# A convolution-and-MLP kernel: the blocked transform becomes a two-stage transform with partition shuffles, the gate becomes one plus a scaled convolution, and the first row passes its norm by itself

## Chip, cores, metric

One core of a Trainium2 chip. Times are microseconds (us) of device time of that core. The experiments ran on two chips: taps_kept, both_half, tail_split and dum_halves on one, the others on another, each beside the kernel before. Words used below: an eviction copies a result of TensorE from PSUM, its output memory, to SBUF, the main memory on the chip; a shuffle is a DMA that moves data between SBUF partitions; a dummy is a matmul whose result nobody reads; TensorE is cold while it runs at half its clock; a row is one of 16 groups of 128 positions. A run is called fast or slow: slow is over 1.5% above the fastest run of the same kernel. A ratio below is the mean time of one kernel's fast runs over the mean of the other's fast runs of the same rounds, so it is not quite the ratio of the medians quoted beside it.

## The reference, cut to what matters

```python
def reference(A_q, A_k, A_v, A_shift_k, A_ssm_k, A_ssm_D, B_x, B_w1, B_b1, B_w2, B_b2):
    # S = 2048, D = 448, F = 1792, bfloat16
    x = A_q
    q = layernorm(x)                                   # over D
    k_shift = sum over 4 taps of shifted k * shift_k   # per channel
    kv = k_shift * v
    y = irfft(rfft(kv, 2S) * rfft(ssm_k, 2S))[:S] + kv * ssm_D   # causal convolution along S
    h = x + q * y
    u = gelu(einsum("bsd,sf->bdf", layernorm(h), w1) + b1)
    return h + transpose(einsum("bdf,fs->bds", u, w2) + b2)
```

The kernel computes the convolution with matmuls against tables of sines, the MLP (which mixes along S) with two chains of 224 matmuls.

## The kernel before

The sequence is cut in 16 tiles of 128 positions and four blocks of 512. Each block is transformed to 512 frequencies, the products for each pair of blocks are summed on TensorE with identity matrices, and each output tile is transformed back, from one block's products or two.

```python
def emit_forward(...):                        # L834: 2 tables x 4 x 4 matmuls per block and signal
    for tab, ... in ((NC_t, ...), (NSf_t, ...)):
        for phi in range(NPHI):
            for tp in range(TPB):
                ... e.matmul(bank(bk), tab[:, tp, 128*phi:128*phi+128], sig[:, tile, :], ...)
            ... e.copy / e.activation(out=dst_ap, in_=bank(bk))     # ScalarE, 448 columns each

def emit_products_b(b):                       # for every block pair c + j = b
    for hf in range(2):
        for c in range(b + 1):
            # four VectorE products, then eight identity matmuls (L908 to L917)
            ... e.matmul(bank(bre), ident,  mset[:, 0, q, :], ...)
            ... e.matmul(bank(bre), nident, mset[:, 1, q, :], ...)
            # [cut]

def emit_inverse_T(T):                        # L945: 8 or 16 matmuls per output tile
    # [cut]

def emit_combine_T(T):
    ... t1s = kv - bank(bk)                   # VectorE, from PSUM (L962)
    ... t2s = t1s * qs2                       # qs2: normalised x, read back from HBM (L964)
    ... hs  = t2s + xs2                       # L966
    # hs goes out to HBM and comes back for the last addition
    # row sums and squares on ScalarE, scale on ScalarE (L970 to L987)
    # [cut]

def emit_gelu(q, fc):                         # two ScalarE passes, three VectorE passes, a sigmoid
    # [cut]
```

## Time and profile before

| | before |
|---|---|
| time, median of 3 runs | 296.19 us (295.44 to 296.56) |
| profiled span | 295.9 us |
| TensorE, VectorE, ScalarE, GpSimd busy | 78%, 60%, 54%, 11% |
| front and convolution, up to the first MLP stretch | 0 to 158 us |
| rest of the inverse, rows, first MLP product, GELU | 158 to 246.5 us |
| second MLP product, store | 246.5 to 295.9 us |

The prediction shows the stretches before 158 us and after 246.5 us. The one between, in the same columns (start:end, length, busy us with instruction counts of TensorE, its weight loads, VectorE, ScalarE and GpSimd, then granted clock, DMA share, GB/s), of the kernel before:

```profile
158.00:246.50 88.50, 73.93 (x344) 34.40 (x345) 38.46 (x111) 46.47 (x100) 10.52 (x26) 0.90 0.55 182
```

The clock of 0.90 and the 14.6 us in which TensorE is idle say that this stretch waits. The chain of waits (start, us, what) says for what, a row that is read back from HBM and weights:

```profile
172.24 9.92 DMA qs<-out_dram
...
215.29 6.37 DMA XB<-in_B_w_dram
...
233.83 4.52 DMA XB<-in_B_w_dram
```

### The profile page before, as it was taken

Reading aid. Unit: us, or ns where it says so; the run is one execution under the profiler, and the core shown is the slowest. Engines: PE = TensorE matmul, PEld = TensorE weight load, DVE = VectorE, ACT = ScalarE, POOL = GpSimd, SP = SyncE. Lnnn points to the kernel's source line nnn. Section 1 sums busy time; section 2 is a strip of 40 time slices with the busy share of each in tenths; the row PEclk is TensorE's granted clock in tenths of the full one; section 3 lists DMA queues with packets and bytes.
Section 4 is the critical chain, followed back from the end, with each engine's and each line's share of the span. In section 5 each row is a group of like instructions: output and inputs, shape, how many; then the busy total and the mean of one; then the engine's idle time right before and its main releaser. Section 6 shows DMA issues by size and latency. Waiting matters only on the chain.

```text
span 295.9 us, 3832 instructions
## 1 busy us (share of the span) xinstructions
PE 229.9 (78%) x1154; PEld 112.8 (38%) x1154; DVE 178.4 (60%) x426; ACT 159.4 (54%) x335; POOL 33.1 (11%) x81
## 2 busy tenths in 40 slices
PE   0024169999779999899928969759929999799995
PEld 0023124455325555445503425325514444345552
DVE  8959986685998974987187772442244124454131
ACT  2389266998753585867682683854656135610000
POOL 6001120000000032221223031321100000000000
PEclk9999999999979999999975989979987999999999
DMA  6721776658043333221220199436984420025322
GB/s 183 193 74 71 224 232 190 199 173 265 7 149 94 111 113 91 78 78 32 65 62 1 47 320 363 113 109 194 328 329 127 141 107 2 0 62 147 105 62 78
DMA packets 28552, 39.36 MB, mean 133 GB/s; under 512 B 3060, under 2 KB 23670, under 8 KB 28532
## 3 DMA queue, kind: packets, MB, share of 16 engines
q1 hardware_dynamic: 22100, 24.44, 27.5%
q10 hardware_dynamic: 6432, 14.68, 14.7%
q8 instruction: 9, 0.15, 0.2%
q14 instruction: 11, 0.09, 0.1%
HBM read 33.61 MB, written 5.51 MB: 132 GB/s over the span
## 4 chain that ended last, share of the span: by engine, by line
PE 44%; DVE 10%; DMA 8%; ACT 5%; issue 2%; POOL 1%; DVEq 1%; SPq 0%; ACTq 0%
PE ps_all L1046 13%; PE ps_all L1063 12%; PE ps_all L945 8%; PE ps_all L834 4%; DMA XB<-in_B_w_dram 4%; DMA qs<-out_dram 3%; PE ps_all L908 2%; PE ps_all L914 2%; PE ps_all L917 2%; PE ps_all L911 2%; DVE XB L888 1%; DVE XB L890 1%; DMA xs<-in_A_q_dram 1%; DVE XB L886 1%; DVE t1s L962 1%
## 5 line engine op out<-in xcount | busy, mean ns | idle before, releaser
L1046 PE MATMUL ps_all<-hn,XB 128*128 128x448 bf16 x224 | 50.3, 379 | 14.1 <-DMA XB<-in_B_w_dram 6.3
L1063 PE MATMUL ps_all<-XB,YB 128*128 128x448 bf16 x224 | 43.6, 353 | 2.5 <-DVE XB L1036 2.5
L1046 PEld LDWEIGHTS ps_all<-hn,XB 128*128 128x128 bf16 x224 | 22.5, 104 | 40.7 <-issue 13.9
L945 PE MATMUL ps_all<-XB,NC_t 128*128 128x448 bf16 x112 | 32.1, 364 | 1.8 <-ACT XB L924 1.1
L945 PE MATMUL ps_all<-XB,NSi_t 128*128 128x448 bf16 x112 | 32.3, 363 | 0.0
L752 PE MATMUL ps_all<-ident,XB 128*128 128x128 bf16 (+1 forms) x64 | 7.0, 293 | 31.7 <-DMA XB<-in_A_ssm_k_dram 17.3
L1063 PEld LDWEIGHTS ps_all<-XB,YB 128*128 128x128 bf16 x224 | 21.4, 98 | 24.3 <-DVE XB L1036 4.6
L834 PE MATMUL ps_all<-kv,NC_t 128*128 128x448 bf16 x64 | 19.9, 366 | 6.9 <-DVE t1s L962 6.9
L1066 DVE SCALAR_TENSOR_TENSOR osb<-ps_all,b2col,hs 128x448 bf16<-128x448 f32 x16 | 10.5, 681 | 21.6 <-PE ps_all L1063 21.6
L924 ACT CAST XB<-ps_all 128x448 bf16<-128x448 f32 x32 | 16.9, 530 | 10.8 <-PE ps_all L911 8.0
L834 PE MATMUL ps_all<-XB,NC_t 128*128 128x448 bf16 x64 | 21.3, 398 | 0.7 <-ACT XB L761 0.7
L840 ACT ACTIVATE YB<-ps_all,sc 128x448 bf16<-128x448 f32 x32 | 18.7, 632 | 4.8 <-PE ps_all L834 4.7
L844 ACT CAST YB<-ps_all 128x448 bf16<-128x448 f32 x32 | 16.6, 534 | 8.4 <-PE ps_all L834 8.3
L834 PE MATMUL ps_all<-kv,NSf_t 128*128 128x448 bf16 x64 | 19.9, 366 | 0.7 <-ACT YB L844 0.7
L790 DVE TENSOR_TENSOR XB<-XB,Wt 128x1792 bf16<-128x1792 bf16 x16 | 17.1, 1079 | 4.9 <-DMA XB<-in_A_k_dram 4.8
L834 PE MATMUL ps_all<-XB,NSf_t 128*128 128x448 bf16 x64 | 19.9, 352 | 0.0
L1029 DVE SCALAR_TENSOR_TENSOR XB<-XB 128x448 bf16<-128x448 bf16 x14 | 8.8, 625 | 15.9 <-ACT XB L1023 8.4
L752 PEld LDWEIGHTS ps_all<-ident,XB 128*128 128x128 bf16 (+1 forms) x64 | 5.7, 139 | 32.8 <-DMA XB<-in_A_ssm_k_dram 18.4
L821 ACT ACTIVATE qs<-xs,nm_x,rs_x 128x448 bf16<-128x448 bf16 x16 | 12.1, 760 | 9.3 <-DVE nm_x L818 9.0
L908 PE MATMUL ps_all<-XB,ident 128*128 128x448 bf16 x40 | 14.5, 364 | 3.1 <-DVE XB L896 2.8
L945 PEld LDWEIGHTS ps_all<-XB,NC_t 128*128 128x128 bf16 x112 | 11.2, 100 | 13.9 <-ACT XB L924 1.5
L970 ACT ACTIVATE junk<-hs 128x448 bf16<-128x448 bf16 x16 | 9.2, 575 | 12.5 <-DVE hs L966 5.6
(103 smaller groups left out, 386.3 us busy)
## 6 DMA issues: line engine op xcount, KB each, us to landing
XB<-in_B_w_dram ACTq DMA_DIRECT2D x32, 224.0 KB, 2.9
YB<-in_B_w_dram ACTq DMA_DIRECT2D x2, 3584.0 KB, 13.6
XB<-in_A_k_dram SPq DMA_DIRECT2D x15, 448.0 KB, 4.0
xs<-in_A_q_dram SPq DMA_DIRECT2D x32, 112.0 KB, 2.2
XB<-in_A_v_dram SPq DMA_DIRECT2D x16, 112.0 KB, 3.2
out_dram<-qs SPq DMA_DIRECT2D x16, 112.0 KB, 1.7
qs<-out_dram SPq DMA_DIRECT2D x16, 112.0 KB, 2.4
out_dram<-hs SPq DMA_DIRECT2D x16, 112.0 KB, 1.9
```

Of the source, the lines that this page charges most:

```text
L752: op("pe", lambda e, dst=dst, slot=slot, tt=tt, w=w: e.transpose(out=dst, in_=knat[0:w, slot, 128 * tt: 128 * tt + 128], identity=ident[0: ...
L790: op(E, lambda e: e.tensor_tensor(out=prod, in0=ktap[:, slot, :, :], in1=Wt, op=ALU.mult), reads=[r_ktap[slot], r_Wt], writes=[r_prod[ei]] ...
L821: op("act", lambda e: e.activation(out=qs[:, slot, :], in_=xs[:, slot, :], func=ACT.Identity, bias=nm_x[:, t:t + 1], scale=rs_x[:, t:t + 1 ...
L834: op("pe", lambda e, bk=bk, lhsT=lhsT, tile=tile, tp=tp: e.matmul(bank(bk), lhsT, sig[:, tile, :], start=(tp == 0), stop=(tp == TPB - 1)), ...
L840: op("act", lambda e, bk=bk, dst_ap=dst_ap, scl=scl: e.activation(out=dst_ap, in_=bank(bk), func=ACT.Copy, scale=scl), reads=[Rbank[bk], r ...
L844: op("act", lambda e, bk=bk, dst_ap=dst_ap: e.copy(out=dst_ap, in_=bank(bk)), reads=[Rbank[bk]], writes=[r_d], n=D)
L908: op("pe", lambda e, bre=bre, mset=mset, q=q, first=first: e.matmul(bank(bre), ident, mset[:, 0, q, :], start=first, stop=False), reads=[r ...
L924: op("act", lambda e, bk=bk, dst=dst: e.copy(out=dst, in_=bank(bk)), reads=[Rbank[bk]], writes=[r_Pst[pslot]], n=D)
L945: op("pe", lambda e, lhsT=lhsT, rhs=rhs, ti=ti: e.matmul(bank(bk), lhsT, rhs, start=(ti == 0), stop=(ti == n - 1)), reads=[r_l, r_r], writ ...
L1046: op("pe", lambda e, q=q, slot=slot, t=t: e.matmul(bank(q), w1s[:, slot, 128 * q: 128 * q + 128], hn[:, t, :], start=(t == 0), stop=(t == ...
L1063: op("pe", lambda e, fc=fc: e.matmul(bank(bk), w2sb[:, fc, 128 * T: 128 * T + 128], gT[:, fc, :], start=(fc == 0), stop=(fc == NFC - 1)), ...
L1066: op("dve", lambda e: e.scalar_tensor_tensor(out=osb[:, ob, :], in0=bank(bk), scalar=b2col[:, T:T + 1], in1=hs2[:, fs, :], op0=ALU.add, op ...
```

## The change

The intent is to take work from TensorE and the round trips from the rows.

- **Transform.** The positions are cut as s = 16 q + r. A first stage multiplies, for each residue r, 128 positions with a sine table (two matmuls, which make 896 columns in PSUM). Shuffle DMAs move the results between partitions inside SBUF, so that the residues lie on the partition axis; a second stage of half-size matmuls (64 stationary columns) finishes the transform. It is taken at odd half frequencies, so that one set of products, one per frequency, serves the causal convolution of the whole sequence, where ten block pairs were needed. The inverse mirrors this: half-size matmuls (64 rows), shuffles, a full-size last stage.
- **Gate.** h - mean = (x - m)(1 + r y) up to a constant of the row, which the following norm removes. So the last stage's PSUM goes through one pass, 1 + scale times convolution, and one combine.
- **First row at once.** Rows 0 and 1 each take a norm of their own, so that row 0 waits for no other; rows 2 to 15 go in pairs.
- Also: GELU is one ScalarE function; a planner chooses the order of instructions and which engine evicts; TensorE runs dummy matmuls in waits.

The diff rewrites nearly the whole file (some 2,000 lines); its core:

```diff
-    for t in range(NT): ... emit_forward / emit_products_b / emit_inverse_T
+def emit_stage1(src, o_src, T, o_T, tag):
+    for r in range(R):
+        for h in range(2):
+            op("pe", ... e.matmul(Pb(b, h), E[:, 2*r + h, :], src[:, r, :], ...))          # L933
+        op("act", ... copy of both banks, 896 columns)                                     # L943
+        for q_, a, b_, j0 in (("pool", 0, 112, 0), ("sp", 112, 128, 14)):
+            op(q_, ... e.dma_start(T[p0:p0 + 29:4, j0:...], WR[a:b_]))                     # L947, shuffle
+def emit_stage2(T, o_T, scale):
+    for jj ...: for h ...:
+        for c in range(2):
+            for par in range(2):
+                op("pe", ... e.matmul(PS[64*par:64*par+64, slot(c), 0:D],
+                                      FW[:, 64*c:64*c+64], T[:, j, h, :], ...))            # L964
+        evac(...)                                    # ScalarE or VectorE, L652 to L656
+def emit_products_i1():
+    op("dve", ... all four products of 448 columns in one tensor_tensor)                   # L1015
+    for t ...: for par in range(2):
+        op("pe", ... e.matmul(Pb(b, par), tab[P, :], M[P, xy, :], ...))   # P: 64 rows, L1027
+    evac(...); shuffle                                                                     # L1037
+def emit_i2():
+    op("pe", ... two matmuls per row)                                                      # L1104
+    op(FX, ... activation(out=A, in_=Pb(b), bias=1.0, scale=r))                            # L1111, gate
+    op("dve", ... A = (X - mean) * A)                                                      # L1118
+    # rows in groups GR = ((0, 1), (1, 1)) + pairs: a group of one takes bn_stats on VectorE,
+    # a group of two row sums with the combine, squares on ScalarE, arithmetic on GpSimd
-    dma(out2d <- hs); ... dma(hs2 <- out2d)
-    # six passes for GELU
+    op("act", ... activation(func=Gelu_apprx_tanh))                                        # L1193
```

## The prediction

> **What bounds the kernel now.** I read the head of the page first, then the stretches view, the groups, and last the chain of waits, where TensorE runs without a stop.
>
> ```profile
> span 295.9 us, 3832 instructions
> PE 229.9 (78%) x1154; PEld 112.8 (38%) x1154; DVE 178.4 (60%) x426; ACT 159.4 (54%) x335; POOL 33.1 (11%) x81
> ```
>
> TensorE is the busiest engine by 50 us, and idle for 66 us. The stretches view (start:end, length, busy us of PE, PEld, DVE, ACT and POOL, then clock, DMA share and GB/s) shows where, cut at the first and last transform and MLP matmuls:
>
> ```profile
> 0.00:40.50 40.50, 7.18 (x66) 5.82 (x66) 34.72 (x69) 21.56 (x39) 6.98 (x20) 1.00 0.54 160
> 40.50:158.00 117.50, 105.33 (x520) 51.20 (x520) 87.27 (x216) 83.06 (x183) 15.56 (x36) 0.96 0.38 114
> ...
> 246.50:292.50 46.00, 43.50 (x226) 21.33 (x223) 16.70 (x31) 8.28 (x15) 0.00 (x0) 1.00 0.23 68
> 292.50:295.90 3.40, 0.00 (x0) 0.00 (x0) 1.22 (x2) 0.00 (x0) 0.00 (x0) 0.81 0.21 68
> ```
>
> VectorE sets the first 40 us (tables, then taps), TensorE most of the convolution and the second MLP product; the last 3.4 us are eviction and store. The time per matmul is not its duration, as matmuls overlap; it comes from the chain:
>
> ```profile
> 261.67 30.83 PE ps_all L1063 x162
> ```
>
> 30.83/162 = 0.190 us. There are 256 forward, 160 identity-sum, 224 inverse and 448 MLP matmuls, 1,088 in all: 207 of the 230 busy us. The groups give the costs that I carry over (count, busy us, mean ns of one):
>
> ```profile
> L790 DVE TENSOR_TENSOR XB<-XB,Wt 128x1792 bf16<-128x1792 bf16 x16 | 17.1, 1079 | 4.9 <-DMA XB<-in_A_k_dram 4.8
> ...
> L924 ACT CAST XB<-ps_all 128x448 bf16<-128x448 f32 x32 | 16.9, 530 | 10.8 <-PE ps_all L911 8.0
> ...
> L962 DVE TENSOR_TENSOR t1s<-kv,ps_all 128x448 bf16<-128x448 bf16 x16 | 9.8, 616 | 2.3 <-PE ps_all L945 2.3
> ...
> L720 ACT ACTIVATE NSi_t<-XB,negpi 128x1024 bf16<-128x1024 f32 x4 | 4.5, 1137 | 2.7 <-DVE XB L719 2.7
> L725 DVE SCALAR_TENSOR_TENSOR XB<-XB 128x1024 f32<-128x1024 f32 x4 | 4.9, 1220 | 0.0
> ```
>
> The reader is to see a large SBUF product, a PSUM eviction on each engine, a table row and [...]VectorE work.
>
> **What the Trainium skill says.** "VectorE: DVE Perf Modes", The perf-mode tier table: a bf16 tensor_tensor in SBUF runs at twice the base rate, fp32 PSUM operands at the base rate. The trace agrees: 390 ns (L966) against 616 ns (L962) for 448 columns. "TensorE: Matmul & The Clock Gate", Part 3: matmuls on different row or column groups of the array run together. Nothing in this trace shows it; the new half-size matmuls rest on it. "DMA: Bandwidth & Descriptors", Why a DMA increments its semaphore by 16 and not by 1: a DMA uses the largest number of engines up to 16 that divides both outer sizes. The shuffles have outer sizes 112 and 8 (16 and 8 for the rest), so 8 engines each; no trace yet. "SBUF — State Buffer", A bandwidth-pool intuition that's wrong: a GpSimd DMA can starve while VectorE runs a two-port copy; the shuffles use that path, but beside them VectorE mostly multiplies or reads PSUM. Not shown here either.
>
> **The change, part by part.** It is nearly a rewrite. The blocked convolution (four blocks, products for every block pair) becomes one transform in two stages of 16 rows, a DMA shuffle between stages, and one product per frequency.
>
> TensorE: the 640 convolution matmuls become 66 first-stage, 68 tap-sum and weight-row, and 32 last-stage ones of full size, plus 128 half-column and 128 half-row ones, which I count in pairs as 128. That is 294 slots or 56 us in place of 122; 97 transposes and 66 clock-keeping dummies fill idle time. The MLP stays at 448. TensorE no longer sets the front; evictions do.
>
> Front, until the last stage can start (my sums):
> - VectorE only: table index work 6.5 (per half one 1,024-column row of 1.22 and about 2 us of faster integer rows); tap products 16 x 1.08 = 17.3; times v from PSUM, 896 columns, [...]1.08, x8 = 8.7; spectrum products 16 x 1.08 = 17.3; row statistics 16 x about 0.77 = 12.3 (estimate from 448 columns at base rate plus a short row); small 2. Sum 64.
> - ScalarE only: sines and table loads 7.7; first-stage evictions of 896 columns, [...]0.90, x32 = 28.9. Sum 37.[...]
> - Either: 48 evictions of 896 columns at a mean near 0.95 (ScalarE 0.90, VectorE 1.08) = 45.6; transposed kernel 6, weight rows 2, inverse tables 3.4. Sum 57.
> Total 158, so 79 us on each engine if both are always busy. I add 3 before either has real work, 3 for the last shuffle, which is a barrier, and 1 net for poor packing less the statistics that can follow later: **86 us**.
>
> In order: first stage of k from about 11 to 27 us, kv done near 41, first stage of u near 43, its shuffle near 46, then 39 us of second stages, products and inverse evictions.
>
> After that TensorE is the bound again: 32 + 448 = 480 matmuls x 0.190 = 91.2. The first normalised row takes a chain of some 4.5 us (0.4 matmuls, 0.7 gate, 0.7 combine, 0.8 statistics, 0.6 power as in L982's 601 ns, 0.5 scale, hops), of which 2 us is other last-stage work: 2.5 lost. Row loop stalls 1. Tail 3.4, as before. Sum **98 us**.
>
> The gate: (x-m)(1 + r y) differs from x + (x-m) r y by a row constant that the norm removes, so two VectorE rows and all q and h round trips through HBM go; per row two PSUM-to-output passes on VectorE (about 1.2 us) and a gate plus square with accumulator read on ScalarE (0.72 + 0.57 + 0.19 = 1.48) remain, under TensorE's 9 x 0.190 = 1.71. Passing the first row through at once brings the first MLP matmul forward by perhaps 1 to 2 us; it is in the 4.5. GELU drops from six passes to one (0.63) and is hidden.
>
> Bytes: the shuffles move 3 x 16 x 128 x 1,792 B = 11 MB in SBUF; HBM traffic falls from 39 to about 24 MB.
>
> 86 + 98 = **184 us**, 0.62 of before.
>
> **Rivals.**
> (a) Shuffles set the front. If 3.67 MB per shuffle went at 100 GB/s, the 37 us would outlast the 15 us of evictions that feed it, three times over: +25 to +60, 210 to 240 us. For: 1,792 B pieces, eight engines, descriptors written by GpSimd. Against: the page's GB/s row reaches 363, so half the engines should still pass 150, and consecutive shuffles can alternate halves.
> (b) Static order and semaphores leave VectorE and ScalarE 85% busy in place of 97%. The old kernel has VectorE at 34.7 of its first 40.5 us. That makes the front 93 to 95 and the time 192.
> (c) Weights come late. Half of w1 and all of w2, 11 MB, may only load after the last shuffle. At 304 GB/s (old trace, 169 to 186 us) they take 36 us and are hidden, as the second product starts some 52 us later; at 192 GB/s (204 to 246 us) 57 us, +5: 189.
> (d) The row loop goes at the pace of evictions, as seven of eight banks hold MLP sums and one is left: 2.2 us a row in place of 1.71 gives +8: 192.
> (e) VectorE rows that need nothing of each other overlap (two of L790 in 2.09, not 2.16) and the row statistics slide behind the last stage: front 80, time 177.
>
> **Range and chances.** (b), (c) and (d) each add 5 to 9 and may come together; (e) takes 7. I give 174 to 198 for 8 in 10. Even (a) stays far below 296, so faster is nearly certain: 0.98 faster, 0.01 same, 0.01 slower.
>
> **What would show it.** Right: last-stage matmuls start at 80 to 94 us; VectorE and ScalarE both over 85% busy from 10 us to there; from then to the end about 98 us with TensorE over 90%; 0.19 us a matmul in the MLP; half-size matmuls at about 0.1 us each. Wrong: VectorE waiting on a DMA for over 8 us in the second stages (a); TensorE waiting for w1 or w2 (c); row period over 2 us (d); half-size matmuls at 0.19, which would cost TensorE 24 us in the front, though under the evictions.

## The result

| | before | after |
|---|---|---|
| time, median of 4 runs each, same rounds | 296.38 us (295.44 to 297.94) | 189.75 us (188.61 to 191.89) |
| ratio of fast runs | | 0.638, 95% interval 0.634 to 0.642 |
| profiled span | 295.9 us | 187.1 us |
| convolution, up to where rows and MLP begin | 158.0 us | 87.7 us |
| rows, first MLP product | 88.5 us | 53.8 us |
| second MLP product and end | 49.4 us | 45.6 us |

The last three rows add up to the spans: of the 108.8 us gained, 70.3 come from the convolution, 34.7 from the rows and the first product, 3.8 from the end. The second stretch is not the same work in both: before, it also held 120 matmuls of the convolution (344 less the MLP's 224), some 23 us at 0.190; after, 32 of them, 6 us. So about half of the 34.7 is the transform's too (an estimate). The rest is near the 20.8 us of DMA waits shown above for the kernel before, which the changed kernel's chain does not have; only the gate's share was tested. One of the four runs of the changed kernel was slow (191.89 us). The result is correct.

The head of the page of the changed kernel:

```profile
span 187.1 us, 2824 instructions
PE 173.9 (93%) x1033; PEld 91.8 (49%) x1033; DVE 110.0 (59%) x181; ACT 97.2 (52%) x141; POOL 72.3 (39%) x176
```

TensorE's 93% is not what it seems. Matmuls overlap, their ends are modelled, and dummies count. The stretches say more (the same columns as before):

```profile
0.00:15.50 15.50, 14.12 (x99) 7.78 (x100) 12.72 (x22) 8.71 (x10) 10.76 (x50) 1.00 0.87 340
15.50:32.80 17.30, 14.15 (x69) 5.79 (x68) 15.43 (x19) 16.15 (x21) 13.85 (x25) 1.00 0.78 222
32.80:50.00 17.20, 16.20 (x93) 6.67 (x95) 14.52 (x15) 14.90 (x18) 13.73 (x24) 1.00 0.74 214
50.00:62.80 12.80, 11.24 (x96) 3.92 (x97) 11.01 (x12) 11.99 (x15) 2.27 (x9) 1.00 0.75 262
62.80:81.10 18.30, 16.69 (x154) 6.59 (x152) 17.62 (x20) 17.01 (x20) 7.82 (x14) 1.00 0.86 280
81.10:87.70 6.60, 6.57 (x34) 3.24 (x34) 6.28 (x21) 0.91 (x1) 6.11 (x13) 1.00 0.61 185
87.70:120.30 32.60, 31.36 (x160) 14.69 (x160) 21.47 (x62) 20.38 (x47) 17.74 (x44) 1.00 0.86 340
120.30:141.50 21.20, 21.20 (x114) 11.05 (x112) 0.00 (x0) 6.50 (x12) 0.00 (x0) 1.00 0.00 0
141.50:183.90 42.40, 42.37 (x224) 32.05 (x222) 10.25 (x15) 0.64 (x1) 0.00 (x0) 1.00 0.11 41
```

Two things are to be seen. From 15.5 to 81.1 us VectorE and ScalarE are both busy nearly all the time, yet so is TensorE: three engines at 82 to 96% in each stretch, and the view does not say which of them holds the others. From 81.1 to 87.7 us ScalarE stands still: it is the last shuffle, and all 34 TensorE instructions in that stretch are dummies. The chain of waits (start, us, what) shows the path from there on:

```profile
62.81 2.50 PE ps L1027 x24
...
81.13 6.61 PE ps L1047 x34
...
87.74 1.70 PE ps L1104 x8
...
120.31 21.19 PE ps L1213 x112
141.49 42.39 PE ps L1223 x224
```

The first line gives 2.50/24 = 0.104 us for a half-size matmul, the last two (21.19 + 42.39)/336 = 0.189 us for a full one. L1047 is the dummies. The groups that took the place of those shown before:

```profile
L943 ACT CAST arena<-ps 128x896 bf16<-128x896 f32 x32 | 26.6, 935 | 3.8 <-PE ps L933 1.9
...
L964 PE MATMUL ps<-arena 128*64 128x448 bf16 x128 | 16.4, 361 | 1.8 <-ACT arena L652 1.0
...
L1015 DVE TENSOR_TENSOR arena<-arena 128x1792 bf16<-128x1792 bf16 x16 | 16.4, 1082 | 0.0
...
L1027 PE MATMUL ps<-arena 64*128 64x448 bf16 x128 | 14.1, 351 | 1.3 <-DVE arena L1015 0.6
```

The mean of 351 ns for a half-size matmul is a duration with a modelled end, not a cost; the spacing of 0.104 us in the chain is the cost. And the shuffles, from the issues part of the page (count, KB each, median us from issue to landing):

```profile
arena<-arena POOLq DMA_DIRECT2D x48, 196.0 KB, 4.9
```

### The profile page after: what moved, and what is told of

The parts are those of the page before. It is cut to its first block, busy times and chain, and to the rows that moved or that the text cites. A ratio compares the mean times of both kernels' runs of the same rounds, so it can differ in the third digit from the quotient of the medians.

```text
span 187.1 us, 2824 instructions
## 1 busy us (share of the span) xinstructions
PE 173.9 (93%) x1033; PEld 91.8 (49%) x1033; DVE 110.0 (59%) x181; ACT 97.2 (52%) x141; POOL 72.3 (39%) x176
## 4 chain that ended last, share of the span: by engine, by line
PE 76%; ACT 8%; DVE 7%; DMA 3%; POOL 3%; issue 2%; ACTq 0%
PE ps L1223 23%; PE ps L1213 11%; PE ps L1203 10%; PE ps L1047 5%; PE ps L1027 5%; ACT arena L652 4%; PE ps L964 4%; DMA arena<-arena 3%; PE ps L1104 3%; PE ps L885 3%; PE ps L914 3%; PE ps L904 3%; POOL arena L947 3%; PE ps L933 3%; DVE arena L1015 2%
## 5 line engine op out<-in xcount | busy, mean ns | idle before, releaser
L1227 DVE SCALAR_TENSOR_TENSOR arena<-ps,arena 128x448 bf16<-128x448 f32 x16 | 10.9, 683 | 56.9 <-PE ps L1223 56.9
L1223 PE MATMUL ps<-arena 128*128 128x448 bf16 x224 | 42.5, 352 | 0.0
L1223 PEld LDWEIGHTS ps<-arena 128*128 128x128 bf16 x224 | 32.3, 144 | 10.1
L943 ACT CAST arena<-ps 128x896 bf16<-128x896 f32 x32 | 26.6, 935 | 3.8 <-PE ps L933 1.9
L652 ACT CAST arena<-ps 128x896 bf16<-128x896 f32 (+1 forms) x26 | 22.0, 908 | 2.6 <-PE ps L868 1.6
L1203 PE MATMUL ps<-arena 128*128 128x448 bf16 x112 | 23.0, 353 | 0.3 <-DVE arena L1159 0.2
L947 POOL DMA_DIRECT2D arena<-arena x32 | 19.2, 603 | 7.1 <-ACT arena L943 4.3
L1213 PE MATMUL ps<-arena 128*128 128x448 bf16 x112 | 21.4, 352 | 0.0
L1193 ACT ACTIVATE arena<-ps,arena 128x448 bf16<-128x448 f32 x14 | 8.2, 641 | 20.1 <-PE ps L1213 14.7
L879 DVE TENSOR_TENSOR arena<-arena 128x1792 bf16<-128x1792 bf16 x16 | 18.3, 1178 | 0.0
L964 PE MATMUL ps<-arena 128*64 128x448 bf16 x128 | 16.4, 361 | 1.8 <-ACT arena L652 1.0
L1111 ACT ACTIVATE arena<-ps,arena 128x448 f32<-128x448 f32 x16 | 11.2, 723 | 12.2 <-PE ps L1104 9.1
L1037 POOL DMA_DIRECT2D arena<-arena x16 | 9.5, 595 | 20.8 <-PE ps L964 15.6
L933 PE MATMUL ps<-arena 128*128 128x448 bf16 x64 | 16.0, 355 | 1.3 <-ACT arena L943 1.3
L885 PE MATMUL ps<-arena 128*128 128x448 bf16 x64 | 14.5, 354 | 2.5 <-ACT arena L943 1.9
L1015 DVE TENSOR_TENSOR arena<-arena 128x1792 bf16<-128x1792 bf16 x16 | 16.4, 1082 | 0.0
L1203 PEld LDWEIGHTS ps<-arena 128*128 128x128 bf16 x112 | 10.9, 98 | 11.1 <-DVE arena L1159 1.3
L1213 PEld LDWEIGHTS ps<-arena 128*128 128x128 bf16 x112 | 11.0, 98 | 10.2
L1027 PE MATMUL ps<-arena 64*128 64x448 bf16 x128 | 14.1, 351 | 1.3 <-DVE arena L1015 0.6
## 6 DMA issues: line engine op xcount, KB each, us to landing
arena<-in_B_w_dram SPq DMA_DIRECT2D x2, 1536.0 KB, 17.2
```

Source lines behind the costliest of these rows:

```text
L652: return e.copy(out=dst(), in_=src())
L879: op("dve", lambda e, W, T=T, i=i, r=r: e.tensor_tensor(out=T[:, i], in0=KH[:, r:r + 4, :], in1=WT, op=ALU.mult), r=[(o_KH + r * DB, 4 * D ...
L885: op("pe", lambda e, W, b=b, T=T, i=i, j=j: e.matmul(Pb(b, i), ID, T[:, i, j, :], start=(j == 0), stop=(j == 3)), r=[(o_ID, 256), (o + (i ...
L933: op("pe", lambda e, W, b=b, r=r, h=h, dl=dl: e.matmul(Pb(b, h), E[:, 2 * r + h, :], src[:, r, :], start=True, stop=not dl), r=[r_E(r), (o ...
L943: return e.copy(out=dst, in_=Ppair(b)) if W == "act" else e.tensor_copy(out=dst, in_=Ppair(b))
L947: shuf[tag + q_ + str(r)] = shuf[tag + q_] = op(q_, lambda e, W, w=w, p0=p0, a=a, b_=b_, j0=j0: e.dma_start(T[p0:p0 + 29:4, j0:j0 + (b_ - ...
```

## The experiments

The changed kernel ran again beside no_wk, no_pairing and gate_undone: 189.67 us median, ratio to before 0.6365 (0.6324 to 0.6406), two of six runs slow. All twelve kernels ran beside the kernel before. The column "against after" is (ratio - 0.6365) x 297.4 us. The intervals of the ratios are 0.003 to 0.008 wide to each side, and both ratios of a difference have one, so differences under 1.4 to 2.7 us, by run, are not told apart from zero: of the table, no_wk, no_pairing, taps_half and tail_split differ. A second caution: the planner chooses the order anew for each kernel. By the traces, VectorE and ScalarE keep their order in taps_kept, both_half, hw_last2 and no_late_dummies, and nearly in no_pairing; in no_wk, gate_undone, norm_pairs, tail_split and taps_half they do not, so what these show is the edit with its new order.

| run | ratio to before | against after |
|---|---|---|
| after_again | 0.6365 | |
| no_wk | 0.6456 | +2.7 us |
| no_pairing | 0.6441 | +2.3 us |
| gate_undone | none (two fast runs only) | about +6 us, by spans |
| norm_pairs | 0.6372 | +0.2 us |
| no_late_dummies | 0.6412 | +1.4 us |
| taps_half | 0.6561 | +5.8 us |
| hw_last2 | 0.6400 | +1.0 us |
| taps_kept | 0.6348 | -0.5 us |
| both_half | 0.6339 | -0.8 us |
| tail_split | 0.6465 | +3.0 us |
| dum_halves | one look | |

> The changed kernel unaltered, beside the variants of this call, so that effects of 1 to 3 us can be read on one chip. Every theory: 188 to 192 us, ratio to before 0.634 to 0.642; last stage starts at 87 to 89 us of the span.

The repeat gave spans from 186.1 to 190.1 us for one and the same kernel. Keep this spread in mind; its likely source appears under no_late_dummies and hw_last2.

### Are VectorE and ScalarE the bound of the front? taps_half, taps_kept, both_half

The main theory, the prediction's: the front is as long as the work of VectorE and ScalarE together. The test halves the tap products.

```diff
-  tensor_tensor(out=T[:, i],      in0=KH[:, r:r+4, :], in1=WT)          # four taps
+  tensor_tensor(out=T[:, i, 0:2], in0=KH[:, r:r+2, :], in1=WT[:, 0:2])  # two taps, wrong on purpose
-  matmul(..., ID, T[:, i, j, :])
+  matmul(..., ID, T[:, i, j % 2, :])
```

> Wrong result on purpose: each tap product of VectorE multiplies two of the four taps (half the elements, TensorE still sums four), which takes some 16 x 0.6 = 9.6 us out of VectorE before 47 us, and nothing else; the order of work is planned anew with the smaller cost. Theory A (the front is bounded by the sum of VectorE and ScalarE, which share the evictions): half of 9.6, so the last stage starts 3.5 to 5 us earlier and the whole is that much shorter. Theory B (latencies and the order of arrival set the front, VectorE's work is beside them): under 1.5 us. Theory C (VectorE alone is the bound): 7 to 9.6 us.

It was 5.8 us slower, which no theory had. The planner had been told the smaller cost and had made another order; the last stage started at 92.7 us, and VectorE was busy for only 4.6 of the 15.1 us from 31.9 to 47. The run says nothing on the bound, and something on how much the order weighs. So the planner's estimate was left as it was, which keeps the order:

> The halved tap products again (wrong result on purpose; 0.617 instead of 1.178 us each in the last run, so 16 x 0.56 = 9 us less of VectorE before 47 us), but with the order of all instructions kept exactly as in the changed kernel, since the run that planned anew came out 6 us longer. Theory A (VectorE and ScalarE together bound the front; with a fixed split ScalarE can't take any of the room that VectorE gets): the last stage starts 1 to 4 us earlier, whole -1 to -4 us. Theory B (neither is the bound; latencies are): within 0.8 us. Theory C (VectorE alone): -7 to -9 us. In all three the 6 us were the new order's; if this run is also longer, they belong to the products themselves.

Result: -0.5 us, and the last stage started at 87.70 us instead of 87.74. VectorE's busy time before 62.8 us fell from 53.7 to 46.2 us, so 7.5 us of work went and nearly nothing came of it. Then ScalarE's evictions of the input's first stage were halved as well:

```diff
   # in the first-stage eviction, on top of the tap products
+  if tag == "u":
+      return e.copy(out=dst[:, 0], in_=Pb(b, 0))     # one bank of two, wrong on purpose
```

> As the run before, and ScalarE's evictions of the first stage of the input copy only one of their two banks (wrong result on purpose, order kept): some 16 x 0.4 = 6.4 us less of ScalarE between 30 and 50 us on top of VectorE's 9. Theory A (the two together bound the front): the last stage starts 5 to 8 us earlier than in the changed kernel, clearly more than with the tap products alone. Theory B (latencies and shuffles bound it): within 1.5 us. Theory C (VectorE alone): no more than the tap products alone gave.

Result: -0.8 us. The evictions fell from 924 to 532 ns (medians). By the busy time of the whole run, 7.8 us were gone from VectorE and 5.2 from ScalarE, some 13 us from the two "binding" engines. Theory A expected the last stage 5 to 8 us earlier; it came 0.3 us earlier, at 87.45 us. (The first stage of both runs happened to start 0.3 to 0.4 us late, too little to matter.) The chain of waits and the stretches of this run:

```profile
8.00 13.09 DMA arena<-in_A_k_dram
...
61.88 1.17 PE ps L1029 x10
...
87.45 1.70 PE ps L1106 x8
```

```profile
32.80:50.00 17.20, 16.63 (x103) 7.35 (x103) 11.89 (x17) 11.35 (x21) 13.24 (x26) 1.00 0.81 225
```

L1029 and L1106 are the inverse product and the last stage, L1027 and L1104 of the changed kernel: the first starts 0.93 us earlier, the second 0.29. In the 17.2 us stretch VectorE and ScalarE are now busy for 11.9 and 11.4 us, a third idle, and TensorE does only slightly more. **Theory A falls for the part of the front up to 50 us**, with this order and this split of the evictions; theory B has the size right. (A plan that makes use of the freed time was not found: taps_half planned anew and was slower.) What holds instead can be read in the changed kernel's chain of waits for that time; no edit tested it:

```profile
23.35 6.47 DMA arena<-arena
...
32.82 0.93 PE ps L885 x4
33.75 1.05 PE ps L933 x5
34.80 0.76 PE ps L885 x4
```

Until 32.8 us it goes through GpSimd's issues of shuffles and the landing of one (6.47 us), which frees a buffer that the next first-stage eviction needs. From 32.8 us TensorE runs tap sums (L885) and first stages (L933) with no gap until 42.3, at 0.19 us each; all TensorE pieces of the chain between 32.8 and 50 add up to some 13 of 17 us. In the run with both halved, the chain before that is the landing of k from HBM at 21.1 us and of one more shuffle at 32.8 us. So the front up to 50 us is held by loads, shuffles and TensorE in turn, with VectorE and ScalarE busy beside them.

From 50 to 81.1 us the chain passes through seven evictions of ScalarE in a row (5.78 us) and VectorE's products, and from 62.8 on VectorE has no more than 0.7 us of room. That the two are the bound there is read, not tested, and TensorE is not out of the path: no_pairing, below, makes only its half-size matmuls dearer, and its last stage starts 1.3 us later.

### Dummies: no_wk and no_late_dummies

The front begins with dummies among the transposes of the convolution kernel. Nine of them are taken away:

```diff
-  N_WZ, N_WI, N_W0, N_WK, N_WJ = 34, 6, 9, 3, 8
+  N_WZ, N_WI, N_W0, N_WK, N_WJ = 34, 6, 9, 0, 8
```

> The nine dummy matmuls placed between the transposes of the kernel sequence are left out (the first nine at the start stay). In the profile the first stage of the sequence only starts at 14.3 us, where I had 11, and the last sixteen transposes wait until 12.4 us for the PSUM bank that the dummies hold. Theory A (the dummies hold a bank back and so delay the start, and the front is a queue of VectorE and ScalarE work that begins with the start): first stage 1.5 to 2.5 us earlier, total 1 to 2.5 us shorter, 187 to 189. Rival B (the dummies keep the TensorE clock up, so without them the early matmuls run slower): granted clock under 0.98 or matmuls over 0.2 us before 30 us, total the same or up to 2 us longer. Rival C (the transposes wait for their loads): no change.

The first stage did start earlier, at 13.5 instead of 14.3 us. But the stretches of this run show the clock:

```profile
0.00:15.50 15.50, 13.05 (x82) 6.93 (x83) 13.08 (x23) 8.02 (x9) 10.78 (x50) 0.94 0.86 344
15.50:31.90 16.40, 15.95 (x74) 6.64 (x75) 13.19 (x16) 15.55 (x19) 13.14 (x23) 0.85 0.70 200
```

0.94 and 0.85, against 1.00 in the changed kernel; matmuls around 14 us took 0.55 us instead of 0.35. The trace's clock records put the half clock at 13.5 to 20.4 us. The first stage gained 0.8 us, and the whole lost 2.7; all six runs were at a mean clock of 0.98 to 0.99. The dummies pay, though the new order may have a part in the 2.7.

A clock that halves is what the Trainium skill describes in "TensorE: Matmul & The Clock Gate", Part 1: The HAM clock gate: the array's clock is halved after an idle window of about 3.4 us, and the window runs freely, so the same kernel may be cold for a while in one run and not in the next. The traces agree with the halving (0.37 instead of 0.19 us a matmul, see hw_last2), with the idle window in no_late_dummies below (half clock 4.2 us after TensorE's last matmul), and with the difference from run to run. TensorE was not idle in no_wk, though: before 13.5 us its timeline shows it waiting for 0.6 us at most. What ran from 4.9 us on were transposes and matmuls of one row; how far these count as work for the clock, no run tests.

The late dummies (34 during the last shuffle, 14 among the first rows) were the other test:

```diff
-  N_WZ, N_WI, N_W0, N_WK, N_WJ = 34, 6, 9, 3, 8
+  N_WZ, N_WI, N_W0, N_WK, N_WJ = 0, 0, 9, 3, 0
```

> Takes away the 48 dummy multiplications behind the inverse products (34 in the 6.6 us in which the last shuffles land, 14 among the first rows); the early ones stay. Theory A (they keep the clock up, as the early ones turned out to do): the granted clock falls under 0.95 somewhere after 81 us and the first last-stage and MLP matmuls run at more than their 0.19 us for a few us: +1.5 to +4 us in all. Theory B (they only fill a wait): no change of the clock after 81 us, the last stage's start stays at 87.7 us (within 0.5), and the whole within 0.7 us of the changed kernel.

```profile
81.10:87.70 6.60, 2.21 (x20) 0.62 (x16) 6.60 (x19) 3.10 (x4) 5.58 (x12) 0.85 0.71 211
87.70:94.50 6.80, 3.83 (x11) 1.60 (x12) 4.05 (x10) 2.79 (x4) 2.10 (x5) 0.50 0.56 166
```

By the clock records the half clock lasts from 85.7 us, 4.2 us after the last inverse product ended (81.5), to 95.9; the last stage of this run starts within it, at 90.67 us, and its longest matmul takes 582 instead of 363 ns. From the start of the last stage to the end it took 100.2 us (99.4 in the changed kernel). Theory A is right in mechanism: the clock falls. Its cost is not told apart from zero: +1.4 us by the ratio, whose interval is 2.4 us to each side; the trace shows 0.8 in the tail. (The profiled run is a slow one, 192.75 us; but the fast runs too list mean clocks of 0.955 and 0.973, where the changed kernel's list 0.98 to 1.00.) The profiled run was longer by 3.8 us mainly for another reason: its first stage started at 16.3 us, 2 us late, in a part of the order that the edit does not touch.

### The last shuffle: hw_last2 and tail_split

The barrier from 81.1 to 87.7 us looked like the easiest gain. First the route: the last four groups' shuffles from SyncE, the small pieces of the last two from ScalarE.

```diff
-  op(q_, lambda ...: e.dma_start(TZ[...], TU[...]))                       # q_: GpSimd, SyncE for the small piece
+  op(("act" if j >= 14 and q_ == "sp" else "sp") if j >= 12 else q_, lambda ...: e.dma_start(TZ[...], TU[...]))
```

> The shuffles of the last four of 16 groups go out from SyncE and (the small pieces of the last two) ScalarE instead of GpSimd; bytes, sources and targets are the same. In the changed kernel the last ones are issued at 82.6 and 83.2 us and land at about 87.3, and nothing but dummies runs on TensorE from 81.1 to 87.7. Theory A (the 4.7 us from issue to landing belong to GpSimd's route): the last stage starts 1 to 2.5 us earlier, whole -1 to -2.5 us. Theory B (the bytes over eight DMA engines take that long by any route): within 0.5 us. Theory C (SyncE's own issues, 0.67 us each, stand in a line): 0.5 to 2 us longer.

The changed kernel's last issues and this run's, each from its timeline (start, us, engine, line):

```profile
82.55 1.27 POOL L1037 DMA_DIRECT2D arena<-arena  x2
```

```profile
79.76 6.88 SPq L1037 DMA_DIRECT2D arena<-arena  x8
...
90.38 1.69 PE L1104 MATMUL ps<-arena 128*128 128x448 bf16 x8 [0.91 <-DMA arena<-arena]
```

In the changed kernel the issues end at 83.82 us and the last stage starts at 87.74, 3.9 us later. Here they end at 86.64 us and it starts at 90.38, 3.7 us later. So the landing does not belong to GpSimd's route (theory A falls), and SyncE's issues, one after the other, end 2.9 us after the last eviction, GpSimd's 1.8 us (theory C): the barrier became 0.9 us longer. The ratio says +1.0 us, which is not told apart from zero.

This profile too has its first stage 2 us late. The chains of the two kernels at the same place in the same order, the changed kernel's first:

```profile
8.08 0.57 PE ps L904 x3
```

```profile
9.56 1.12 PE ps L904 x3
```

Three dummies (L904) take 0.19 us each in one run and 0.37 in the other: TensorE is still cold there, though the clock column says 1.00 for the stretch. The column counts as 1.00 whatever lies before the trace's first clock record, which stands at 10.6 us here and at 4.9 us in the changed kernel. As TensorE is the chain from 1.4 to 15.5 us, the whole front starts later: nine profiled runs have that record at 4.1 to 6.1 us and their first stage at 14.1 to 14.7, this one and no_late_dummies have 10.6 and 16.3. This is the likely source of the spread of one and the same kernel; only profiled runs show it, so for the other runs it is an inference.

Second, in the last pair one eviction went to VectorE instead of both to ScalarE in a row:

```diff
   evac(..., bs[h], 2 * D,
+       engs=FX if jj < 7 else ("dve",) if h == 0 else ("act",))
```

> In the last pair of groups one eviction of the inverse products goes to VectorE and one to ScalarE, where the changed kernel has both on ScalarE, one after the other (0.93 us each), while VectorE takes row statistics that nobody waits for yet. Theory A (the last shuffles then go out 0.9 us earlier and the last stage starts that much earlier): -0.5 to -1 us. Theory B (the shuffles' own queue and landing time swallow it): 0, within 0.4 us. Theory C (the statistics that VectorE does later delay the first rows, or the order that is planned around it is worse): +0.5 to +2 us.

+3.0 us, slower than theory C allowed. ScalarE's last eviction waits for TensorE's last inverse product anyway (1.1 us) and ended at 82.05 us, where it ended at 82.01 before; GpSimd's issues ended only 0.3 us earlier, at 83.51. The last stage started 5.1 us after that instead of 3.9, at 88.56 us; and with the new order of VectorE's row statistics the rows and the first half of the first product took 34.1 instead of 32.6 us. The wait for ScalarE had only covered a wait for TensorE, so theory A falls, and the new order cost more than theory C gave it. Why the landing took 1.2 us longer is open.

### Half-size matmuls: no_pairing and dum_halves

The prediction rested on two half-size matmuls running side by side. The order was changed so that neighbours use the same half:

```diff
-  for c in range(2):
-      for par in range(2):
+  for par in range(2):
+      for c in range(2):            # second stage: 2 in a row on one half
-  for t, (tab, xy) in enumerate(...):
-      for par in range(2):
+  for par in range(2):
+      for t, (tab, xy) in enumerate(...):   # inverse: 4 in a row on one half
```

> The half-size matmuls of the second stages and of the inverse products are ordered so that matmuls on the same half of the array follow each other, with no neighbour on the other half. Same instructions, same numbers. Theory A (halves run beside each other only when neighbours use different halves; TensorE has slack in the front): half-size matmuls go from 0.11 us to about 0.19 us each, 256 of them, some 20 us more TensorE work before 88 us; TensorE had some 15 us of real slack there, so total +3 to +9 us. Rival B (TensorE sets the front, as the page's 93% busy and 76% of the chain suggest): +18 to +22 us. Rival C (pairing does nothing, or rests on distance in the queue and not on neighbours): 0.11 us each as before, total the same.

+2.3 us, of which the profiled run shows 1.3 by the start of its last stage (89.07 us), with the cost only partly lost. The line of this run's chain that answers to the 2.50 us above, and one of a group of eight; then such a group of the changed kernel:

```profile
63.19 3.22 PE ps L1027 x24
...
66.68 0.87 PE ps L1027 x8
```

```profile
65.58 0.87 PE ps L1027 x8
```

0.134 instead of 0.104 us in the stretch of 24, not 0.19, and no loss at all in the group of eight. In such groups the starts still come in pairs, 13 ns apart (3 ns in the changed kernel). Either pairing is not needed, or the hardware still finds pairs. So the 34 late dummies were used as a bench: 20 matmuls on one half of the columns (L1048), then 20 that alternate (L1055).

```diff
-  for i in range(34): e.matmul(Pb(b), FW, ET...)
+  for i in range(20): e.matmul(PS[0:64, ...], FW[:, 0:64], ET...)
+  for i in range(20): h = i % 2; e.matmul(PS[64*h:64*h+64, ...], FW[:, 64*h:64*h+64], ET...)
```

> The 34 dummies while the last shuffles land become 20 matmuls that all use the same half of the array's columns (64 stationary columns, the same 64 output partitions), then 20 that alternate between the two halves; 448 moving columns each, as in the second stage. One look, for the spacing of their starts. Theory A (two half-size matmuls run side by side only if neighbours in the order use different halves): the 20 of one half start 0.17 to 0.19 us apart (3.6 us for all), the alternating ones about 0.10 us (2 us). Theory B (a half-size matmul takes half the time whatever its neighbour): both about 0.10 us. Theory C (no gain from half size): both about 0.19 us. The second run with the pairing undone lost only 1 to 2 us, which speaks against A, but its runs of one half were only two to four long.

Its timeline of TensorE (start, us from first start to last end, count):

```profile
80.33 3.59 PE L1048 MATMUL ps<-arena 128*64 128x448 f16 x18
83.57 0.38 PE L1055 MATMUL ps<-arena 128*64 128x448 f16 x1
83.76 0.35 PE L1048 MATMUL ps<-arena 128*64 128x448 f16 x1
...
83.95 0.35 PE L1048 MATMUL ps<-arena 128*64 128x448 f16 x1
83.98 2.21 PE L1055 MATMUL ps<-arena 128*64 128x448 f16 x18
```

Less the last one's 0.35 us, the starts are (3.59 - 0.35)/17 = 0.191 us apart on one half, and (2.21 - 0.35)/17 = 0.109 us when alternating. **Theory A is right: half size alone gains nothing, only the pairing does.** The lines in the middle suggest why undoing it cost so little: in the program all 20 of L1048 stand before L1055, but the first L1055 starts at 83.57 us, ahead of the last two L1048. So a matmul overtakes two waiting ones (by their spacing one of the free half, though the trace does not print the half), which would be enough to find pairs where only two to four of one half stand in a row, as the paired starts of no_pairing bear out. (Its single time of 187.57 us is inside the changed kernel's spread; nothing is concluded from it.)

### The gate and the first row: gate_undone and norm_pairs

The gate's folding was undone: the PSUM pass only scales, and a further VectorE row adds x.

```diff
-  A = 1 + r * conv ;  A = (x - m) * A  (row sums taken here)
+  A = r * conv     ;  A = (x - m) * A
+  A = 1.0 * A + x                       # scalar_tensor_tensor, row sums taken here
```

> The gate part alone is undone: the gate only scales by r, the combine makes (x-m) r y, and one more VectorE row adds x (0.68 us each, 16 of them, +10.9 us of VectorE work after 88 us). Theory A (in the row loop TensorE is the bound at 1.7 us a row, VectorE has 1.3 us a row in the changed kernel, and with the added row about 2.0): the row loop stretches by 16 x 0.25, total +3 to +6 us. Rival B (VectorE has room, all hidden): under +1 us. Rival C (the VectorE chain per row is the bound already): +9 to +11 us.

Only two of six runs were fast, so there is no interval. Its best run had a span of 193.1 us at a clock of 1.0, against 186.9 us at 1.0 for the changed kernel: about +6 us. From its groups, the added row (L1120) and the first half of the first product (L1206, and what its waits were for), and from its chain the second half (L1216):

```profile
L1206 PE MATMUL ps<-arena 128*128 128x448 bf16 x112 | 23.0, 353 | 4.6 <-DVE arena L1162 4.4
...
L1120 DVE SCALAR_TENSOR_TENSOR arena<-arena 128x448 f32<-128x448 f32 x16 | 9.6, 618 | 0.0
```

```profile
131.35 18.57 PE ps L1216 x98
```

9.6 us of VectorE were added (16 passes that overlap a little), and TensorE now waits for the scaled row (L1162). The profiled run was cold in its front, but its tail can be compared: from the start of the last stage (90.35 us) to the end of the first product (149.92) it took 59.6 us, where the changed kernel took 53.8 (87.74 to 141.49): +5.8 us. So VectorE has little room in the row phase, and the folded gate is worth roughly two thirds of the work it saves, the new order of instructions included. The size is uncertain by a few us; the direction is not.

The first row's own norm was undone alone:

```diff
-  GR = ((0, 1), (1, 1)) + tuple((2 + 2 * g, 2) for g in range(7))
+  GR = tuple((2 * g, 2) for g in range(8))
```

> Undoes one named part: rows 0 and 1 share one norm chain again, with sums taken by ScalarE and GpSimd arithmetic, instead of row 0 passing through its own norm at once. Theory A (the first row's own norm lets the first multi-layer product start earlier, and TensorE is then the bound to the end): the first such product starts 1 to 2 us later than the 94.5 us of the changed kernel, and the whole is +1 to +2 us. Theory B (TensorE catches nothing up because the row pace, not the start, sets the first half): 0, within 0.5 us. If both effects are there, the start moves by 1 to 2 us and the whole by less than half of that.

+0.2 us, which by the noise could still be 2; the traces tell more. Its last stage started at 88.49 us and the first MLP matmul at 95.9, that is 7.4 us after (5.9 in the changed kernel, 93.6 less 87.7). But the chain of this run shows the second half at

```profile
120.87 21.19 PE ps L1211 x112
```

120.87 less 88.49 is 32.4 us; the changed kernel took 120.31 less 87.74, 32.6 us. The 1.5 us of earlier start are given back later in the row phase: what ends it is when the last row is ready, not when the first one is. So theory B, by the chain of one run.

## Why the prediction was right, and where it was not

Predicted 184 us, range 174 to 198; measured 189.75. The time was inside the range, and the spread of the two halves close: front 86 predicted, 87.7 measured; tail 98 predicted, 99.4 measured. Point by point:

1. **The work left TensorE, right.** The full-size spacing of 0.190 us carried over (0.189). The half-size spacing of about 0.1 us was right (0.104), and dum_halves shows that it rests on the pairing.
2. **"TensorE no longer sets the front; evictions do": this step failed, up to 50 us.** Taking some 13 us from VectorE and ScalarE moved the start of the last stage by 0.3 us, where the step asks for 5 to 8. By the chains, loads, the shuffle buffers and TensorE hold the front there in turn. The number 86 came out by luck, because two errors cancel. VectorE and ScalarE did 77.6 + 69.7 = 147 us of work before 87.7 us (158 predicted, of which some 4 slid behind the last stage), and were idle for about 28 us together instead of 14. The stretches show where: 9.6 us up to 15.5 us (6 predicted), 12.6 from there to 81.1 (2 predicted), 6.0 during the last shuffle (6 predicted). The sign of being right, both over 85% busy from 10 us on, held for VectorE (89%) and just failed for ScalarE (84%).
3. **"3 before either has real work": too small for ScalarE.** It was idle for 6.8 of the first 15.5 us, VectorE for 2.8. The first stage started at 14.3 us, not 11: TensorE's own chain of dummies, transposes and weight rows lies there, and can be cold.
4. **"3 for the last shuffle": it took 6.6 us,** and VectorE filled 6.3 of them with row statistics, which were in the sum anyway. The shuffles land 3.6 to 5.5 us after issue, by GpSimd as by SyncE. Neither another route nor an earlier eviction shortened it.
5. **The tail, right.** 91.2 us of matmuls were predicted; they took 27.4 (144 x 0.190) and 63.6 us. The row phase lost 5.2 us where 3.5 were foreseen; the end took 3.2 (3.4). That the first row's own norm would be worth "1 to 2 us" at the first matmul is right for the start (1.5 us) and wrong for the time (0.2).
6. **Rivals.** (a), shuffles at 100 GB/s, is wrong as put: VectorE does not wait for them for 8 us. In small it is right between 16 and 33 us, where a shuffle's landing is in the chain. (b), engines 85% busy in place of 97%, came half true (89% and 92% from 15.5 to 81.1 us), but names the idle time, not its cause; its sum is wrong too, since 79/0.85 = 93 leaves out the 7 us that the prediction adds to 79, and with them the front would be 100. (c), late weights, did not occur: 120.3 and 141.5 us show no wait. (d), the pace of rows, did not occur in the changed kernel, and appears as soon as VectorE gets one more row pass (gate_undone). (e) came true in its parts, not in the time: five spectrum products took 5.09 us in place of 5 x 1.08, and a quarter of the row statistics came after 87.7 us, which is some of the work that was missing from the 158. (Its front of 80 makes 178, not 177.)
7. The remaining 5.75 us between 184 and 189.75 are 1.7 in the front, 1.4 in the tail, 1.8 between span and measured time, which the prediction did not add (188.93 against 187.1 us for the profiled run), and about 0.8 of runs with a longer span.

Left open: what bounds the front from 16 to 33 and from 50 to 81 us by experiment, how the gain of the row stretch is shared by tested parts, and whether the front's cold starts explain all of the spread.

## What to carry to other kernels

Two engines that are both 90% busy are not thereby the bound: keep the order of instructions, take work from them, and see whether the end moves; here some 13 us of removed work gave 0.8, which is not told apart from zero. When a planner or scheduler chooses the order, a smaller cost may give a worse order (5.8 us slower with less work), so an experiment must fix the order first. Half-size matmuls pay only in pairs on different halves, and dummies that look like waste may be what keeps the clock at full speed. A clock column can read 1.00 because nothing was recorded yet: check it by the spacing of equal matmuls.

## What the Trainium skill lacked or had wrong

- "TensorE: Matmul & The Clock Gate", Part 3: Packing small matmuls says that matmuls start and end strictly in program order. In the trace of dum_halves a matmul of L1055 starts at 83.57 us, ahead of two of L1048 (83.76 and 83.95 us) that stand before it in the program.
- The same page and part gives no case of undone pairing. Here: 0.191 us with 20 in a row on one half, 0.134 us with four in a row in a stretch of 24 (0.109 in groups of eight), 0.104 to 0.109 us alternating.
- "DMA: Bandwidth & Descriptors", Anatomy of one DMA — SWDGE (gpsimd) path, gives about 2.0 us plus bytes over 436 GB/s, for 196 KB an estimate of 2.5 us. The shuffles within SBUF, several in flight at a time, took 3.1 to 7.5 us in the first stage (median 5.2) and 3.6 to 5.5 us in the last (median 4.7); sent from SyncE the last ones landed no sooner (3.7 against 3.9 us after the last issue).
- No page says how many matmuls among transposes keep the clock up. With nine dummies among the transposes the changed kernel's trace shows no half clock in the front after 4.9 us; without them (no_wk) it lasts from 13.5 to 20.4 us, and all six runs have a mean clock of 0.98 to 0.99.
